# Attention followed by a token and channel mixer: the transposed q and k leave PSUM in another order of elements

## The chip, the cores and the metric

One core of a Trainium2 chip runs the whole program. The metric is the device time of one execution in microseconds (us); less is better. TensorE (PE) multiplies, VectorE (DVE) and ScalarE (ACT) read its results out of PSUM and do the elementwise work, GpSimd (POOL) works in SBUF only, and SyncE (SP) issues the DMAs.

## What is computed

For 8 batches and 8 heads, 576 tokens, head size 64: causal attention with a decay, and then a mixer over tokens and over channels on the joined heads (512 channels).

```python
s_pos = np.maximum(s, 0.0)
cum = np.cumsum(s_pos, axis=-1)
bias = -(cum[:, :, :, None] - cum[:, :, None, :])
scores = np.where(causal, -1e9, q @ k.T / 8 + np.minimum(bias, 0.0))
attn = softmax(scores)
x = (attn @ v)                       # heads joined: (8, 576, 512)
h = relu(x.T @ w_tok1) @ w_tok2      # tokens mixed, 256 wide
u = x + h.T
out = u + relu(u @ w_ch1) @ w_ch2    # channels mixed, 1536 wide
```

## The kernel before, in words

The work falls into 32 pairs of heads (8 batches of 4 pairs), and a mixer per batch.

**A pair.** One DMA (line 405) loads q, another k, for two heads: token 6p + r lies in partition p at place r, so 96 partitions hold six tokens each. POOL (line 412; for batch 0 also ACT, 416, or DVE, 414) casts them to bf16. Six PE transposes of 96x96 (line 436) write the transposed k side by side into one PSUM tile, psc: column r * 96 + p holds token 6p + r. A copy brings it into kT in order of tokens, by ACT (line 446) or DVE (line 448). The same is done for q, except that two copies of 64 partitions each (line 456 on ACT, line 458 on DVE) put the two heads into the two halves of qT, whose other parts are zero. The second copy does not start before the first has ended. Then come the scores: nine matmuls of kT against qT (line 473) in seven pieces, each in a psc tile, an exp per part of a piece on ACT (line 481), a mask on the diagonal blocks on DVE (line 489), 30 small matmuls with v (line 510, AV below), a reciprocal (517) and a scaling (522) on DVE. Tiles psc_113 to psc_115 are three PSUM banks shared by the transposes and the score pieces; kT, qT and E have three tiles each.

**A mixer.** Matmuls of lines 603 and 623 with transposes of line 642 mix tokens; lines 669 (with a relu on ACT, 676, or DVE, 678) and 688 (with an add on DVE, 699) mix channels. They use three other PSUM banks, pmx_118 to pmx_120.

**The order.** Nothing is scheduled at run time. Every step is given to a planner with the engines that may do it and a duration per engine; the planner takes the steps one by one, always the one that can start first by its own clock, with ties (within 0.03 us) settled by a priority in which the token mixer (0) comes ahead of attention (1) and that ahead of the channel mixer (2). For PE, attention's AV comes ahead of scores and those ahead of transposes. The planner picks the engine, too: every copy of q and k may go to ACT or DVE. What it picks is written out as the fixed order of each engine's queue, and an engine whose next instruction has to wait holds up all behind it. The planner's duration for one copy of q or k is 0.55 us on ACT (`c_act(576)`) and 0.67 us on DVE (`c_dve(576)`); for a cast on POOL it is 0.10 us and 1.5 ns per element.

Of the kernel before, what the change touches and what calls it, by code (L numbers as in the profile page):

```python
# [9 lines left out]
BF16 = mybir.dt.bfloat16  # L10
# [190 lines left out]
def c_act(n, bias=False):  # L201
    occ = 0.07 + n * 0.000833 + (0.093 if bias else 0.0)
    return occ, occ + 0.22


def c_dve(n, two=False):
    occ = 0.07 + n * (0.00053 if two else 0.00104)
    return occ, occ + 0.22


def c_pool(n, per=0.0022):
    occ = 0.10 + n * per
    return occ, occ + 0.25
# [3 lines left out]
def kernel(  # L217
# [12 lines left out]
    nc = tc.nc  # L230

    B, H, S, D = q.shape
# [8 lines left out]
    R = 6  # L241
    PR = S // R
# [49 lines left out]
    P = Plan()  # L292
    count = [0]

    def seq():
        count[0] += 1
        return count[0]
# [73 lines left out]
    def stage_v(b):  # L371
        vf, vp = Buf(r_vf), Buf(r_vp)
        vbuf[b] = vp
        for c in range(NJ):
            n = min(128, S - c * 128)

            def load(c=c, n=n):
                nc.sync.dma_start(out=vf.t[0:n, c, :, :],
                                  in_=v[b, :, c * 128 : c * 128 + n, :].rearrange("h p d -> p h d"))
            P.op({"SP": (0.6, 0, load)}, writes=[(vf, c)], prio=seq(), dma=1024 * 0.02 / 16 * n / 128)  # L380
        for c in range(NJ):
            n = min(128, S - c * 128)

            def mul(eng, c=c, n=n):
                eng.tensor_tensor(  # L385
                    out=vp.t[0:n, c, :, 0:D], in0=vf.t[0:n, c, :, :],
                    in1=wT[0:n, c, b * H : b * H + H].unsqueeze(2).to_broadcast([n, H, D]), op=ALU.mult)
            alts = ({"DVE": (*c_dve(512), lambda mul=mul: mul(nc.vector))} if b == 0 else
                    {"POOL": (*c_pool(512), lambda mul=mul: mul(nc.gpsimd))})
            P.op(alts, reads=[(vf, c), "wT"], writes=[(vp, c)], prio=b * 10 + 5 if b else 0)  # L390

        def ones():
            nc.gpsimd.tensor_copy(out=vp.t[:, 0 : NJ - 1, :, D], in_=wT[:, 0 : NJ - 1, b * H : b * H + H])
            nc.gpsimd.tensor_copy(out=vp.t[0:64, NJ - 1, :, D], in_=wT[0:64, NJ - 1, b * H : b * H + H])
        P.op({"POOL": (0.5, 0.7, ones)}, reads=["wT"], writes=[(vp, "w")], prio=b * 10 + 5)
# [3 lines left out]
    def stage_qk(b, h):  # L399
        for buf, src in (("k", k), ("q", q)):  # L400
            f, n = Buf(r_qf), Buf(r_qn)
            qkn[(buf, b, h)] = n

            def load(f=f, src=src):
                nc.sync.dma_start(out=f.t[:, :, :, :].rearrange("p e r d -> p e (r d)"),
                                  in_=src[b, h : h + 2, :, :].rearrange("e (p r) d -> p e (r d)", r=R))
            P.op({"SP": (0.6, 0, load)}, writes=[(f, 0)], prio=seq(), dma=192 * 0.064 / 16)

            def cast(e, f=f, n=n):
                i = f.t[:, :, :, :].rearrange("p e r d -> p r e d")  # L410
                if e == 0:
                    nc.gpsimd.tensor_copy(out=n.t[:, :, :, :], in_=i)
                elif e == 1:
                    nc.vector.tensor_copy(out=n.t[:, :, :, :], in_=i)
                else:
                    nc.scalar.copy(out=n.t[:, :, :, :], in_=i)
            alts = {"POOL": (*c_pool(768, 0.0015), lambda cast=cast: cast(0))}
            if b == 0:
                alts["DVE"] = (*c_dve(768), lambda cast=cast: cast(1))
                alts["ACT"] = (*c_act(768), lambda cast=cast: cast(2))  # L420
            P.op(alts, reads=[(f, 0)], writes=[(n, 0)], prio=b * 10 + h)
# [3 lines left out]
    def pair(b, h):  # L425
        pi = b * H + h
        qn, kn = qkn[("q", b, h)], qkn[("k", b, h)]
        qT, kT, E = Buf(r_qT), Buf(r_kT), Buf(r_E)
        pr = (1, pi)
        for nat, dst in ((kn, kT), (qn, qT)):  # L430
            pt = Buf(r_sc, False)

            def tr(nat=nat, pt=pt):
                o = pt.t[:, :].bitcast(BF16)
                for r in range(R):
                    nc.tensor.transpose(out=o[:, r * PR : (r + 1) * PR],
                                        in_=nat.t[:, r, :, :].rearrange("p e d -> p (e d)"), identity=ident[0:PR, 0:PR])
            P.op({"PE": (R * 0.045, R * 0.045 + 0.3, tr)}, reads=[(nat, 0)], writes=[(pt, 0)], holds=[dst], prio=(1, pi, 2))

            def un(p0, p1, pt=pt):  # L440
                return pt.t[p0:p1, :].bitcast(BF16)[:, 0 : R * PR].rearrange("d (r p) -> d r p", r=R)
            if dst is kT:
                def evk(eng, un=un):
                    o = kT.t[:, 0:S].rearrange("d (p r) -> d r p", r=R)
                    if eng == 0:
                        nc.scalar.copy(out=o, in_=un(0, 128))
                    else:
                        nc.vector.tensor_copy(out=o, in_=un(0, 128))
                P.op({"ACT": (*c_act(576), lambda evk=evk: evk(0)), "DVE": (*c_dve(576), lambda evk=evk: evk(1))},
                     reads=[(pt, 0)], writes=[(kT, 0)], prio=1)  # L450
            else:
                for hh in range(2):
                    def evq(eng, hh=hh, un=un):
                        o = qT.t[hh * 64 : hh * 64 + 64, hh, :].rearrange("d (p r) -> d r p", r=R)
                        if eng == 0:
                            nc.scalar.copy(out=o, in_=un(hh * 64, hh * 64 + 64))  # L456
                        else:
                            nc.vector.tensor_copy(out=o, in_=un(hh * 64, hh * 64 + 64))  # L458
                    P.op({"ACT": (*c_act(576), lambda evq=evq: evq(0)),
                          "DVE": (*c_dve(576), lambda evq=evq: evq(1))},  # L460
                         reads=[(pt, 0)], writes=[(qT, hh)], prio=1)
        for pc, piece in enumerate(PIECES):
# [14 lines left out]
            for (jc, a, e, c0) in cols:  # L477
# [6 lines left out]
                if a == jc * 128:  # L484
                    n = min(128, S - a)
# [46 lines left out]
    def load_w(slot, n, dma_fn, dst, key, us):  # L532

        st = stage[slot]
        P.op({"SP": (0.6, 0, lambda: dma_fn(st))}, writes=[("st", slot)], prio=seq(), dma=us)

        def cast(e):
            for (d, i) in dst(st):
                if e == 0:
                    nc.gpsimd.tensor_copy(out=d, in_=i)  # L540
                elif e == 1:
                    nc.vector.tensor_copy(out=d, in_=i)
                else:
                    nc.scalar.copy(out=d, in_=i)
        P.op({"POOL": (*c_pool(n, 0.0015), lambda: cast(0)), "DVE": (*c_dve(n), lambda: cast(1)),
              "ACT": (*c_act(n), lambda: cast(2))}, reads=[("st", slot)], writes=[key], prio=3)

    def load_tok():
# [19 lines left out]
    def load_ch1(mc):  # L568
        load_w((2, 3, 0, 1)[mc], DC,
               lambda st: nc.sync.dma_start(out=st[:, :], in_=moe_w_ch1[mc * 128 : mc * 128 + 128, :]),  # L570
               lambda st: [(wc1[:, mc, :], st[:, :])], ("wc1", mc), 2.1)
# [84 lines left out]
    def chan(b, u, us, uT):  # L656
# [26 lines left out]
        for c in range(5 if odd else 4):  # L683
# [20 lines left out]
            P.op({"SP": (0.6, 0, st)}, reads=[(o, 0)], prio=0, dma=128 * 0.088 / 16)  # L704

    stage_qk(0, 0)
    stage_v(0)
    for h in range(2, H, 2):
        stage_qk(0, h)
    load_tok()  # L710
    for i in range(4):
        load_ch1(i)
    stage_qk(1, 0)
    stage_v(1)
    for i in range(4):
        load_ch2(i)
    for h in range(2, H, 2):
        stage_qk(1, h)
    for b in range(2, B):
        stage_v(b)  # L720
        for h in range(0, H, 2):
            stage_qk(b, h)
# [46 lines left out]
```

## Time and profile before

| | |
|---|---|
| two runs | 476.28 and 479.09 us, median 477.68 |
| profiled execution, its own time | 477.95 us |
| its span in the trace | 476.3 us, 7665 instructions |
| busy: PE, ACT, DVE, POOL | 370.4, 310.5, 251.4, 94.0 us |
| granted TensorE clock, mean | 0.903 of full speed |

The span is what the trace covers; 1.65 us of the execution lie outside it. Busy shares are averages over two unlike stages: up to about 346 us pairs and mixers are interleaved, after that only mixers are left. Which wait ends last in a stage is told by the chain of work, which is followed back from the last instruction.

### The profile page before, as it was taken

What the parts mean: (1) busy time and instruction counts of PE and PEld (TensorE: products, weight loads), DVE (VectorE), ACT (ScalarE), POOL (GpSimd) and SP (SyncE); (2) the same over time, 40 slices, a digit from 0 to 9 for tenths busy, and PEclk for the clock granted to TensorE, in tenths of its full rate; (3) what the DMA queues carried; (4) which work ended last, traced back from release to release, by engine and by line L of the source; (5) the groups of instructions that cost most, each with busy time, mean ns of one, the idle gap of its engine ahead of it and who ended that gap; (6) DMA issues with size and microseconds to landing.
All of it is one profiled execution on the core that took longest, in us unless ns stands there. A gap on an engine that the chain in (4) does not pass through costs nothing.

```text
span 476.3 us, 7665 instructions
## 1 busy us (share of the span) xinstructions
PE 370.4 (78%) x2949; PEld 206.2 (43%) x2949; DVE 251.4 (53%) x498; ACT 310.5 (65%) x504; POOL 94.0 (20%) x129
## 2 busy tenths in 40 slices
PE   1547648686596696597677586788999999999996
PEld 1324314343343554363424343434764446544562
DVE  7958886664555877672557746735603213130102
ACT  4796776898668987786868769856651516325250
POOL 1453821332143215214304302100000000000000
PEclk9997969997788977787979979968999999999999
DMA  9999999272314806501322300001002010020202
GB/s 190 307 241 247 311 196 279 50 164 76 98 45 123 184 15 142 108 27 51 114 77 94 101 1 3 22 23 45 1 6 106 1 60 30 23 88 1 88 17 95
DMA packets 59172, 45.86 MB, mean 96 GB/s; under 512 B 39296, under 2 KB 52160, under 8 KB 59136
## 3 DMA queue, kind: packets, MB, share of 16 engines
q1 hardware_dynamic: 59136, 45.38, 36.4%
q8 instruction: 23, 0.38, 0.3%
q14 instruction: 13, 0.11, 0.1%
HBM read 35.93 MB, written 9.44 MB: 95 GB/s over the span
## 4 chain that ended last, share of the span: by engine, by line
PE 56%; ACT 21%; DVE 18%; issue 4%; ACTq 0%; DVEq 0%
PE pmx_119 L669 7%; PE pmx_120 L688 7%; PE pmx_118 L669 7%; PE pmx_118 L688 6%; PE pmx_120 L669 6%; PE pmx_119 L688 6%; ACT qT_79 L456 5%; ACT qT_81 L456 4%; DVE qT_79 L458 4%; ACT qT_80 L456 4%; PE psc_113 L473 3%; DVE qT_80 L458 3%; PE psc_114 L473 3%; DVE qT_81 L458 3%; PE psc_115 L473 2%
## 5 line engine op out<-in xcount | busy, mean ns | idle before, releaser
L669 PEld LDWEIGHTS <-wc_67 128*128 128x128 bf16 x576 | 58.6, 103 | 45.9 <-issue 10.6
L688 PEld LDWEIGHTS <-gb_108 128*128 128x128 bf16 x240 | 23.6, 100 | 27.3 <-issue 2.4
L489 DVE TENSOR_TENSOR E_86<-E_86,keep 128x256 bf16<-128x256 bf16 (+1 forms) x55 | 21.3, 405 | 18.2 <-ACT E_86 L481 18.1
L688 PEld LDWEIGHTS <-ga_107 128*128 128x128 bf16 x192 | 19.6, 104 | 25.2 <-issue 8.3
L489 DVE TENSOR_TENSOR E_87<-E_87,keep 128x256 bf16<-128x256 bf16 (+1 forms) x50 | 15.3, 321 | 25.4 <-ACT E_87 L481 25.2
L669 PE MATMUL pmx_119<-uTb_106,wc_67 128*128 128x320 bf16 x136 | 26.5, 321 | 0.0
L473 PEld LDWEIGHTS <-kT_83 128*128 128x128 bf16 x99 | 10.1, 110 | 36.9 <-issue 30.5
L385 POOL TENSOR_TENSOR vp_91<-vf_89,wT 128x512 bf16<-128x512 f32 (+1 forms) x20 | 20.5, 1046 | 26.5 <-PE pav_117 L510 22.5
L473 PEld LDWEIGHTS <-kT_84 128*128 128x128 bf16 x90 | 9.4, 112 | 36.5 <-issue 29.7
L669 PE MATMUL pmx_118<-uTb_106,wc_67 128*128 128x320 bf16 x132 | 25.0, 315 | 0.0
L473 PEld LDWEIGHTS <-kT_82 128*128 128x128 bf16 x99 | 9.6, 107 | 31.7 <-issue 26.3
L688 PE MATMUL pmx_118<-wc_68,gb_108 128*128 128x512 bf16 x84 | 22.5, 413 | 0.0
L473 PE MATMUL psc_113<-qT_80,kT_83 128*128 128x512 bf16 (+1 forms) x30 | 11.9, 397 | 13.5 <-ACT qT_80 L456 9.1
L669 PE MATMUL pmx_120<-uTb_106,wc_67 128*128 128x320 bf16 x116 | 21.8, 313 | 0.0
L489 DVE TENSOR_TENSOR E_85<-E_85,keep 128x256 bf16<-128x256 bf16 (+1 forms) x55 | 15.8, 305 | 10.2 <-ACT E_85 L481 10.1
L473 PE MATMUL psc_113<-qT_81,kT_84 128*128 128x128 bf16 (+2 forms) x35 | 10.7, 373 | 13.5 <-ACT qT_79 L456 7.3
L458 DVE COPY qT_80<-psc_115 64x576 bf16<-64x576 bf16 x7 | 14.6, 2080 | 11.9 <-ACT qT_80 L456 9.0
L688 PE MATMUL pmx_120<-wc_68,ga_107 128*128 128x512 bf16 x84 | 20.5, 380 | 0.0
L676 ACT ACTIVATE ga_107<-pmx_120 128x512 bf16<-128x512 f32 x15 | 9.0, 602 | 17.5 <-PE pmx_120 L669 17.3
L688 PE MATMUL pmx_120<-wc_68,gb_108 128*128 128x512 bf16 x84 | 19.9, 379 | 0.0
L473 PE MATMUL psc_115<-qT_81,kT_84 128*128 128x512 bf16 (+2 forms) x31 | 10.7, 376 | 11.9 <-DVE qT_81 L458 7.0
L676 ACT ACTIVATE gb_108<-pmx_120 128x320 bf16<-128x320 f32 x24 | 10.5, 437 | 13.9 <-PE pmx_120 L669 11.9
(285 smaller groups left out, 986.6 us busy)
## 6 DMA issues: line engine op xcount, KB each, us to landing
gb_108<-in_moe_w_ch_dram SPq DMA_DIRECT2D x6, 768.0 KB, 9.5
vf_88<-in_v_dram SPq DMA_DIRECT2D x16, 256.0 KB, 5.3
vf_89<-in_v_dram SPq DMA_DIRECT2D x16, 256.0 KB, 6.1
qkf_69<-in_k_dram SPq DMA_DIRECT2D x11, 288.0 KB, 3.7
qkf_70<-in_q_dram SPq DMA_DIRECT2D x11, 288.0 KB, 4.2
qkf_71<-in_k_dram SPq DMA_DIRECT2D x11, 288.0 KB, 4.4
qkf_72<-in_q_dram SPq DMA_DIRECT2D x11, 288.0 KB, 4.6
qkf_73<-in_k_dram SPq DMA_DIRECT2D x10, 288.0 KB, 5.3
```

Of the source, the lines that this page charges most:

```text
L385: eng.tensor_tensor(out=vp.t[0:n, c, :, 0:D], in0=vf.t[0:n, c, :, :], in1=wT[0:n, c, b * H : b * H + H].unsqueeze(2).to_broadcast([n, H, D ...
L456: nc.scalar.copy(out=o, in_=un(hh * 64, hh * 64 + 64))
L458: nc.vector.tensor_copy(out=o, in_=un(hh * 64, hh * 64 + 64))
L473: nc.tensor.matmul(out=o[:, :, c0 : c0 + e - a], lhsT=kT.t[:, jc * 128 : jc * 128 + 128], rhs=qT.t[:, :, a:e], start=True, stop=True)
L489: nc.vector.tensor_tensor(out=E.t[:, :, d0 : d0 + n], in0=E.t[:, :, d0 : d0 + n], in1=keep[:, 0:n].unsqueeze(1).to_broadcast([128, 2, n]), ...
L669: nc.tensor.matmul(out=pm.t[:, 0 : e - a], lhsT=wc1[:, m, cc * 128 : cc * 128 + 128], rhs=uT.t[:, m, a:e], start=(m == 0), stop=(m == NMC ...
L676: lambda cc=cc, pm=pm, a=a, e=e: nc.scalar.activation(out=g.t[:, cc, a:e], in_=pm.t[:, 0 : e - a], func=AF.Relu),
L688: nc.tensor.matmul(out=pm.t[:, :], lhsT=g.t[:, cc, c * 128 : c * 128 + 128], rhs=wc2[:, cc, :], start=(cc == 0), stop=(cc == NCC - 1))
```

## The change

The copies of lines 446, 448, 456 and 458 walk over the same elements in another order. Before, the six runs of 96 columns are read as they lie in PSUM, and each element is written six elements (12 bytes) behind the last one. After, kT and qT are written from the first token to the last without gaps, and PSUM is read with a step of 96 elements (192 bytes), six reads per token group. Three of the planner's durations for POOL change with it: the casts of q, k and of the weights from 1.5 to 1.0 ns per element, the products with v from 2.2 to 1.9.

```diff
-                    {"POOL": (*c_pool(512), lambda mul=mul: mul(nc.gpsimd))})
+                    {"POOL": (*c_pool(512, 0.0019), lambda mul=mul: mul(nc.gpsimd))})
...
-            alts = {"POOL": (*c_pool(768, 0.0015), lambda cast=cast: cast(0))}
+            alts = {"POOL": (*c_pool(768, 0.0010), lambda cast=cast: cast(0))}
...
-                return pt.t[p0:p1, :].bitcast(BF16)[:, 0 : R * PR].rearrange("d (r p) -> d r p", r=R)
+                return pt.t[p0:p1, :].bitcast(BF16)[:, 0 : R * PR].rearrange("d (r p) -> d p r", r=R)
             if dst is kT:
                 def evk(eng, un=un):
-                    o = kT.t[:, 0:S].rearrange("d (p r) -> d r p", r=R)
+                    o = kT.t[:, 0:S].rearrange("d (p r) -> d p r", r=R)
...
-                        o = qT.t[hh * 64 : hh * 64 + 64, hh, :].rearrange("d (p r) -> d r p", r=R)
+                        o = qT.t[hh * 64 : hh * 64 + 64, hh, :].rearrange("d (p r) -> d p r", r=R)
...
-        P.op({"POOL": (*c_pool(n, 0.0015), lambda: cast(0)), "DVE": (*c_dve(n), lambda: cast(1)),
+        P.op({"POOL": (*c_pool(n, 0.0010), lambda: cast(0)), "DVE": (*c_dve(n), lambda: cast(1)),
```

Since the planner sees other durations, it writes out another order from the second pair on. On DVE, in the second and third pair of batch 0 (tiles numbered 80 and 81 are their qT, E_86 the second pair's exponentials, w_0 a weight of the token mixer), this is the difference:

```order
-L458 COPY qT_80<-psc_114 64x6x96
-L448 COPY kT_84<-psc_115 128x6x96
+L458 COPY qT_80<-psc_114 64x576
+L448 COPY kT_84<-psc_115 128x576
+L458 COPY qT_81<-psc_113 64x576 x2
 L489 TENSOR_TENSOR E_86<-E_86,keep 128x2x128
 L542 CAST w_0_64<-ga_107 128x1024
 L542 CAST w_0_64<-ga_107 64x256
-L489 TENSOR_TENSOR E_86<-E_86,keep 128x2x128 x3
-L489 TENSOR_TENSOR E_86<-E_86,keep 128x2x64
-L458 COPY qT_81<-psc_114 64x6x96
-L458 COPY qT_79<-psc_113 64x6x96
```

Both halves of the third pair's q now stand on DVE, ahead of the second pair's masks; before, one half stood behind them and the other on ACT.

On ACT, near row 142 of its queue, where one pair's last exp (E_86) and the next pair's exps (E_87) stand, before:

```order
L481 ACTIVATE E_86<-psc_113 128x2x64
L456 COPY qT_81<-psc_115 64x6x96
L446 COPY kT_82<-psc_114 128x6x96
L456 COPY qT_79<-psc_113 64x6x96
L481 ACTIVATE E_87<-psc_115 128x2x256
```

And at the same row in the changed kernel:

```order
L481 ACTIVATE E_86<-psc_114 128x2x64
L481 ACTIVATE E_87<-psc_115 128x2x256
L481 ACTIVATE E_87<-psc_113 128x2x256
L481 ACTIVATE E_87<-psc_114 128x2x64
L481 ACTIVATE E_87<-psc_114 128x2x192
```

The three copies that stood between the two pairs' exps have moved: the half of q that belongs to E_87 stands ten rows earlier, the k and q of the pair after it eight rows later. Over the program, ACT has 22 copies of k and 37 of q before, 23 and 32 after; DVE has 10 and 27 before, 9 and 32 after. On PE the number of channel-mixer matmuls behind the last AV is the same in both, 352 of line 669 and 276 of line 688.

## Rows read from the trace of the kernel before

**Rows 1.** Chain that ended last, 0 to 346 us, by line
```profile
by line: ACT qT_79 L456 6.6%; ACT qT_81 L456 6.1%; DVE qT_79 L458 5.4%; ACT qT_80 L456 5.4%; issue 4.6%; PE psc_113 L473 4.4%; PE pmx_119 L669 4.3%; DVE qT_80 L458 4.3%; PE pmx_118 L669 4.3%; PE psc_114 L473 3.9%; DVE qT_81 L458 3.5%; PE ps
```
**Rows 2.** Chain in order of time: start us, us, what
```profile
31.10 1.92 ACT kT_82 L446
...
121.81 0.27 PE psc_115 L436 x6
122.08 0.02 issue
122.11 2.12 ACT qT_81 L456
124.23 0.02 issue
124.25 2.07 DVE qT_81 L458
126.32 0.03 issue
126.35 2.07 DVE qT_79 L458
...
128.51 2.07 ACT qT_79 L456
...
289.29 0.66 ACT kT_83 L446
```
**Rows 3.** Windows: each engine's busy time (and count), granted clock, DMA share, GB/s
```profile
12.00:48.00 36.00, 21.25 (x206) 12.24 (x206) 27.25 (x52) 28.54 (x47) 15.00 (x17) 0.91 1.13 266
...
200.00:250.00 50.00, 36.86 (x315) 20.21 (x315) 25.70 (x59) 38.55 (x60) 11.71 (x15) 0.80 0.23 68
...
346.00:476.30 130.30, 125.28 (x701) 66.19 (x698) 26.87 (x42) 46.69 (x95) 0.00 (x0) 1.00 0.12 47
```
**Rows 4.** Lines 456, 458, 446: copies by tile, ns min/median/max, first and last start
```profile
L456 ACT COPY qT_81<-psc_115 x8: 2061/2092/2121, 58.3 to 307.3; 64x576 bf16<-64x576 bf16 x8
...
L458 DVE COPY qT_80<-psc_115 x7: 2069/2081/2096, 49.1 to 324.2; 64x576 bf16<-64x576 bf16 x7
...
L446 ACT COPY kT_83<-psc_113 x8: 2057/2116/2339, 20.3 to 289.3; 128x576 bf16<-128x576 bf16 x8
```
**Rows 5.** Other reads of PSUM, same columns
```profile
L650 ACT COPY uTa_105<-pmx_119 x3: 585/592/667, 57.4 to 396.7; 128x512 bf16<-128x512 bf16 x3
...
L652 DVE COPY uTb_106<-pmx_120 x4: 418/422/425, 106.2 to 371.6; 128x512 bf16<-128x512 bf16 x4
...
L676 ACT ACTIVATE gb_108<-pmx_118 x25: 437/437/653, 171.2 to 459.2; 128x320 bf16<-128x320 f32 x25
...
L676 ACT ACTIVATE ga_107<-pmx_119 x11: 597/597/605, 78.4 to 435.5; 128x512 bf16<-128x512 f32 x11
...
L678 DVE TENSOR_SCALAR gb_108<-pmx_118 x8: 478/488/492, 162.3 to 339.4; 128x320 bf16<-128x320 f32 x8
...
L678 DVE TENSOR_SCALAR ga_107<-pmx_119 x4: 684/688/692, 74.4 to 286.2; 128x512 bf16<-128x512 f32 x4
...
L517 DVE RECIPROCAL rc_96<-pav_117 x16: 183/185/196, 19.8 to 340.0; 128x5 f32<-128x5 f32 x16
```
**Rows 6.** Windows over stretches in which only copies stand on the chain
```profile
9.20:13.27 4.07, 0.77 (x5) 0.71 (x6) 3.26 (x2) 1.96 (x2) 0.00 (x0) 1.00 1.17 233
122.11:130.58 8.47, 3.00 (x48) 1.86 (x45) 5.22 (x6) 6.08 (x3) 2.37 (x3) 0.82 0.45 137
...
324.24:328.42 4.18, 2.50 (x14) 1.26 (x13) 3.29 (x3) 3.90 (x2) 0.00 (x0) 1.00 0.16 62
```
**Rows 7.** Chain again: groups of four PE matmuls at two durations
```profile
70.99 1.71 PE pmx_118 L669 x4
...
153.20 1.07 PE pmx_119 L669 x4
...
204.30 1.07 PE pmx_118 L669 x4
...
215.85 2.09 ACT kT_82 L446
...
218.56 1.71 PE pmx_118 L688 x4
...
224.54 0.86 PE pmx_118 L688 x4
...
316.71 1.71 PE pmx_119 L688 x4
```

## The prediction

> **What bounds the kernel now.** I read the chain of waits first, cut at 346 us, because the last AV ends near there and the order of PE behind it is the same in both kernels. Up to that point the copies of q hold 18.1% of the chain on ACT and 13.2% on DVE [rows 1]: of 346 us that is 62.6 and 45.7 us. The copies of k hold little, because they run beside the transposes of q: ten pieces, the first and last of which are shown [rows 2], 11.2 us on ACT and 5.2 on DVE. Together 124.7 us of the span hang on copies, and none lies behind 329 us.
>
> The pieces in order of time show how [rows 2]: six transposes of 0.27 us, then one half of q on ACT, the other half on DVE, then the next pair's halves, 8.47 us without a piece of PE. The windows come next. The stretch behind 346 us is PE's: 125.28 of 130.30 us busy at the full clock [rows 3]. Nothing in the change reaches it, so it stays 130 us. In the interleaved part no engine is full (200 to 250 us: PE 36.9, ACT 38.6, DVE 25.7 of 50 us), so it is latency that bounds it, and the longest latency is the copy.
>
> **What one copy costs now.** All 96 copies have medians of 2.06 to 2.3 us, the same on ACT and DVE, for 64 and for 128 partitions [rows 4]. The engines' own rates differ: ACT reads 320 columns of PSUM in 437 ns and 512 in 597, 0.83 ns a column over 170 ns; DVE takes 488 and 688, 1.04 ns a column over about 155 [rows 5]. At these rates 576 columns are 0.65 us on ACT and 0.75 on DVE. Since both engines come to 3.3 ns an element instead, the limit is no engine but the access. Of its two sides the read is innocent: line 650 reads bf16 from PSUM just as these copies do, without a step, and its 512 columns take 592 ns [rows 5]. What is left is the write with a step of 12 bytes.
>
> **What it will cost.** The new write has no gaps, which line 650 prices. The new read takes one element per 192 bytes of PSUM, which no long instruction of this trace does. From below: ACT 0.65 us; DVE 0.46 us if it takes two elements at a time as line 652 does (422 ns for 512) [rows 5], which I do not count on since neighbours in the new order are not neighbours in PSUM. From above: the reciprocal of line 517 reads five elements 264 bytes apart and takes 185 ns [rows 5], 25 ns more than five columns at DVE's rate; put wholly on the step, that is 5 ns an element more, and a copy would be 0.75 + 2.88 = 3.6 us. I take 0.65 and 0.75 us, since a reciprocal can well be slower than a copy by 25 ns of its own, and the bulky rows all lie at the engines' rates.
>
> [...]
>
> **The sum.** It is made against the profiled execution's own 477.95 us, which is 0.27 above the median of the two runs.
> - Copies on ACT: the chain has 62.6 + 11.2 = 73.8 us of them; a mean copy of 2.15 us becomes 0.65, so 70% goes: -51.5.
> - Copies on DVE: 45.7 + 5.2 = 50.9 us; 2.09 becomes 0.75, so 64% goes: -32.6. That makes 393.9.
> - PE works under the copies, too, and this cover shrinks. The copies on the chain form 26 stretches (three are shown, the first and the last among them [rows 6]), 124.8 us long, with 47.7 us of PE in them. Shortened to 0.325 of its length, a stretch like 122.11 to 130.58 leaves 2.75 us for 3.00 us of PE. Where PE's work is the longer, PE becomes what is late next; over the 26 stretches this adds up to +11.0.
> - [...] Granted clock is 0.80 from 200 to 250 us, and 1.00 once PE no longer waits [rows 3]. With waits of 1.4 us where 4.2 stood I count these groups at the full level: 10 x 0.85 + 9 x 0.53 = -13.3. Between none of it and, with the score matmuls that lie among them, twice as much.
> - The order: the half of q that DVE now does without a handover from ACT, and the copies that no longer stand between two pairs' exps, save or cost a wait here and there; the hold-ups by a queue's head scale with the copies, which the planner now prices nearly right (0.55 and 0.67 us). I put this at 0, with 10 us either way.
> - The durations for POOL change no instruction. POOL has 94 us of work off the chain, and its casts are prepared ahead: 0.
>
> 393.9 + 11.0 - 13.3 = 391.6; I say 391. Its own range is 368 (the clock twice, the order at its best) to 412.
>
> **The rivals.**
> 1. The read with a step pays half of what the write paid: a mean copy of 1.4 us. The chain holds 124.7 / 2.1 = 59 copies, each 0.7 shorter: -41, so 437. For it speaks that the step is far greater than before; against it that nothing in the trace shows a read from PSUM above the engines' rates, save 25 ns of a reciprocal. [...]
> 2. The front runs out of data. From 12 to 48 us the DMA engines are full (266 GB/s [rows 3]); six of the 26 stretches, 28.7 us of copies, lie before 85 us. If loads take the place of what goes there, some 19 us are given back: 410.
> 3. The change does not do what it says, since the read pays all that the write paid: 2.1 us a copy, no change, 478. The order alone is left, and the copies are as badly priced as before.
> 4. The other side: a read with a step is dearer than a write with one. By the reciprocal's 5 ns a copy is 3.6 us, and 59 x 1.5 us = 89 come on top: 566. It decides from a mean copy of 2.25 us on, where 59 x 0.16 passes 2%, about 9.6 us, which is what a measurement of this kernel tells from no change.
>
> **How the numbers follow.** Forecast 0.63, rival 1 0.18, rival 2 0.08, rival 3 0.05, rival 4 0.06. Faster by over 2% is the sum of the first three, 0.89; within 2% rival 3, 0.05; slower 0.06. The range runs from 360, below the forecast's own as the clock's and the order's bounds allow, to 440, which takes in rivals 1 and 2; rivals 3 and 4 and the tails are left out.
>
> **What would show it.** Lines 446 and 456 near 0.65 us and lines 448 and 458 near 0.75; copies under 15% of the chain up to the last AV, with PE's matmuls and the exps of line 481 in their place; the last AV near 261 us and 130 us of mixers behind it; a granted clock above 0.9 from 50 us on. A copy above 1 us would prove the price wrong; copies at 0.7 us with the last AV behind 285 us would prove the chain wrong.

## The result and the profile after

The changed kernel takes 374.48 us (373.98 and 374.98), the one before 477.68: a ratio of 0.784, 95% interval 0.773 to 0.795. The profiled execution took 374.98 us, its span is 373.2. The forecast was 391 us with a range of 360 to 440; 87 us of gain were expected and 103 came.

The copies, by tile, with their shortest, median and longest duration in ns, answer to [rows 4]:

```profile
L446 ACT COPY kT_84<-psc_113 x5: 632/632/639, 114.1 to 210.5; 128x576 bf16<-128x576 bf16 x5
...
L456 ACT COPY qT_79<-psc_114 x7: 615/633/634, 9.1 to 221.9; 64x576 bf16<-64x576 bf16 x7
...
L458 DVE COPY qT_79<-psc_114 x9: 736/750/760, 9.8 to 221.1; 64x576 bf16<-64x576 bf16 x9
```

2.08 us have become 0.63 on ACT and 0.75 on DVE: each engine is back at its own rate [rows 5], to within 20 ns of the two values that the forecast took. The windows answer to [rows 3]:

```profile
12.00:48.00 36.00, 28.34 (x301) 16.79 (x299) 28.08 (x67) 28.70 (x64) 20.12 (x24) 0.95 1.11 275
48.00:100.00 52.00, 46.21 (x469) 27.17 (x469) 39.38 (x90) 39.45 (x86) 21.11 (x25) 0.97 1.14 249
...
150.00:200.00 50.00, 48.15 (x501) 28.41 (x500) 36.71 (x88) 38.51 (x89) 22.79 (x29) 1.00 0.37 113
...
243.00:373.20 130.20, 124.15 (x692) 65.26 (x690) 26.87 (x42) 45.76 (x93) 0.00 (x0) 0.99 0.12 47
```

The last AV now ends near 239 us instead of 343. Behind it stand 134 us of mixers, where 133 stood before: the whole gain lies in the interleaved part. PE was busy for 37 of 50 us there (200 to 250 us [rows 3]); now it is busy for 48 (150 to 200 us), with the clock granted in full (1.00, against 0.80 in those 50 us of before). The chain up to 243 us, by line, answers to [rows 1], and the four pieces of DMA on it to nothing that was there before:

```profile
by line: DMA gb_108<-in_moe_w_ch_dram 5.6%; PE pmx_118 L688 5.0%; PE psc_114 L473 4.6%; PE pmx_120 L669 4.6%; PE psc_115 L473 4.5%; PE pmx_119 L669 4.4%; PE pmx_120 L688 4.3%; PE psc_113 L473 4.0%; DMA qkf_73<-in_k_dram 3.9%; PE pmx_118 L66
...
26.06 6.15 DMA vf_89<-in_v_dram
44.65 7.30 DMA gb_108<-in_moe_w_ch_dram
52.15 9.52 DMA qkf_73<-in_k_dram
72.49 6.40 DMA gb_108<-in_moe_w_ch_dram
```

No copy is left among the large shares; summed over all pieces the copies hold 25 us of 243, where it was 125 of 346. The largest shares are now PE's matmuls and, up to 79 us, 29.4 us of loads. In microseconds PE's pieces have shrunk as well, from 150 to 135.

### The profile page after: what moved, and what is told of

The parts are those of the page before. It is cut to its first block, busy times and chain, and to the rows that moved or that the text cites. A ratio compares the mean times of both kernels' runs of the same rounds, so it can differ in the third digit from the quotient of the medians.

```text
span 373.2 us, 7668 instructions
## 1 busy us (share of the span) xinstructions
PE 340.0 (91%) x2949; PEld 198.0 (53%) x2949; DVE 207.2 (56%) x498; ACT 228.3 (61%) x504; POOL 93.5 (25%) x129
## 4 chain that ended last, share of the span: by engine, by line
PE 68%; DVE 13%; DMA 8%; ACT 7%; issue 2%; POOL 1%; SPq 0%; ACTq 0%; DVEq 0%; POOLq 0%
PE pmx_118 L688 9%; PE pmx_120 L688 8%; PE pmx_120 L669 8%; PE pmx_119 L669 7%; PE pmx_118 L669 7%; PE pmx_119 L688 6%; DMA gb_108<-in_moe_w_ch_dram 4%; PE psc_114 L473 3%; PE psc_115 L473 3%; PE psc_113 L473 3%; DMA qkf_73<-in_k_dram 3%; PE pmx_119 L603 2%; PE pav_117 L510 2%; DVE ua_101 L630 2%; PE pav_116 L510 2%
## 5 line engine op out<-in xcount | busy, mean ns | idle before, releaser
L669 PEld LDWEIGHTS <-wc_67 128*128 128x128 bf16 x576 | 55.7, 98 | 37.4 <-issue 1.9
L688 PEld LDWEIGHTS <-gb_108 128*128 128x128 bf16 x240 | 23.1, 98 | 26.3 <-issue 0.4
L688 PEld LDWEIGHTS <-ga_107 128*128 128x128 bf16 x192 | 18.3, 97 | 19.8 <-issue 0.5
L489 DVE TENSOR_TENSOR E_86<-E_86,keep 128x256 bf16<-128x256 bf16 (+1 forms) x55 | 18.6, 355 | 11.3 <-ACT E_86 L481 10.9
L489 DVE TENSOR_TENSOR E_87<-E_87,keep 128x256 bf16<-128x256 bf16 (+1 forms) x50 | 18.9, 391 | 9.7 <-ACT E_87 L481 9.2
L489 DVE TENSOR_TENSOR E_85<-E_85,keep 128x256 bf16<-128x256 bf16 (+1 forms) x55 | 22.3, 425 | 3.6 <-ACT E_85 L481 3.3
L669 PE MATMUL pmx_119<-uTb_106,wc_67 128*128 128x320 bf16 x132 | 23.3, 299 | 0.0
L669 PE MATMUL pmx_120<-uTb_106,wc_67 128*128 128x320 bf16 x132 | 23.3, 299 | 0.0
L669 PE MATMUL pmx_118<-uTb_106,wc_67 128*128 128x320 bf16 x120 | 21.2, 299 | 0.0
L688 PE MATMUL pmx_118<-wc_68,ga_107 128*128 128x512 bf16 x84 | 20.6, 379 | 0.0
L688 PE MATMUL pmx_118<-wc_68,gb_108 128*128 128x512 bf16 x84 | 20.1, 379 | 0.0
L688 PE MATMUL pmx_120<-wc_68,gb_108 128*128 128x512 bf16 x84 | 19.9, 379 | 0.0
L676 ACT ACTIVATE gb_108<-pmx_120 128x320 bf16<-128x320 f32 x26 | 11.4, 437 | 13.9 <-PE pmx_120 L669 11.9
L676 ACT ACTIVATE gb_108<-pmx_119 128x320 bf16<-128x320 f32 x27 | 11.9, 439 | 12.9 <-PE pmx_119 L669 10.7
L669 PE MATMUL pmx_120<-uTa_105,wc_67 128*128 128x512 bf16 x76 | 19.5, 379 | 0.0
L481 ACT ACTIVATE E_85<-psc_115 128x128 bf16<-128x128 f32 (+2 forms) x37 | 15.8, 462 | 3.7 <-PE psc_115 L473 3.7
L481 ACT ACTIVATE E_86<-psc_114 128x512 bf16<-128x512 f32 (+2 forms) x36 | 15.8, 467 | 3.3 <-PE psc_114 L473 2.8
L481 ACT ACTIVATE E_85<-psc_113 128x512 bf16<-128x512 f32 (+2 forms) x31 | 15.3, 511 | 3.4 <-PE psc_113 L473 3.4
L688 PE MATMUL pmx_119<-wc_68,gb_108 128*128 128x512 bf16 x72 | 16.8, 379 | 0.0
L481 ACT ACTIVATE E_86<-psc_115 128x512 bf16<-128x512 f32 (+2 forms) x28 | 14.1, 520 | 3.9 <-PE psc_115 L473 3.9
```

Of the source, the lines that this page charges most:

```text
L481: nc.scalar.activation(out=E.t[:, :, d0 : d0 + e - a], in_=i[:, :, c0 : c0 + e - a], func=AF.Exp, scale=0.125)
L489: nc.vector.tensor_tensor(out=E.t[:, :, d0 : d0 + n], in0=E.t[:, :, d0 : d0 + n], in1=keep[:, 0:n].unsqueeze(1).to_broadcast([128, 2, n]), ...
L669: nc.tensor.matmul(out=pm.t[:, 0 : e - a], lhsT=wc1[:, m, cc * 128 : cc * 128 + 128], rhs=uT.t[:, m, a:e], start=(m == 0), stop=(m == NMC ...
L676: lambda cc=cc, pm=pm, a=a, e=e: nc.scalar.activation(out=g.t[:, cc, a:e], in_=pm.t[:, 0 : e - a], func=AF.Relu),
L688: nc.tensor.matmul(out=pm.t[:, :], lhsT=g.t[:, cc, c * 128 : c * 128 + 128], rhs=wc2[:, cc, :], start=(cc == 0), stop=(cc == NCC - 1))
```

## The experiments

The change has two parts which the diff mixes: the access of the copies, and three planner durations that set a new order. The planner is not told how the copies walk, so the parts can be had one by one. Four runs shared one chip; their ratios are against the kernel before on that chip.

**The access alone, in the order of before.**

```diff
-                    {"POOL": (*c_pool(512, 0.0019), lambda mul=mul: mul(nc.gpsimd))})
+                    {"POOL": (*c_pool(512), lambda mul=mul: mul(nc.gpsimd))})
...
-            alts = {"POOL": (*c_pool(768, 0.0010), lambda cast=cast: cast(0))}
+            alts = {"POOL": (*c_pool(768, 0.0015), lambda cast=cast: cast(0))}
...
-        P.op({"POOL": (*c_pool(n, 0.0010), lambda: cast(0)), "DVE": (*c_dve(n), lambda: cast(1)),
+        P.op({"POOL": (*c_pool(n, 0.0015), lambda: cast(0)), "DVE": (*c_dve(n), lambda: cast(1)),
```

> The new access with the planner's old durations for POOL, so that the order of every engine is the one of before. If the access makes the whole gain and the order nothing: 372 to 380 us, copies at 0.63 and 0.75 us. If the 17 us by which the change beat the forecast come from the new order: 388 to 395 us, the sum of the forecast without its order term (391).

Measured: 371.68 us, ratio 0.778 (0.775 to 0.781). The access makes the whole gain in an order that is word for word that of before. So the surplus over the forecast is not the order's. This run is also the cleanest pair to before, since nothing but the copies differs. Its busy times, its chain up to 240 us by line (buffer numbers left out), and two of its windows:

```profile
PE 342.2 (92%) x2949; PEld 198.5 (53%) x2949; DVE 213.4 (57%) x498; ACT 227.4 (61%) x504; POOL 96.4 (26%) x129
...
by line: PE psc L473 13.9%; PE pmx L669 13.3%; PE pmx L688 12.2%; DVE E L489 9.5%; PE pav L510 7.6%; PE pmx L603 7.3%; DVE qT L458 5.1%; ACT E L481 4.4%; ACT qT L456 2.9%; PE psc L436 2.8%; DVE ua L630 2.5%; issue 2.0%; DVE x L522 2.0%; DVE
...
150.00:200.00 50.00, 48.44 (x517) 29.06 (x515) 38.79 (x91) 38.64 (x89) 21.98 (x28) 1.00 0.38 110
...
240.00:372.10 132.10, 127.09 (x714) 67.46 (x711) 26.87 (x42) 48.18 (x98) 0.00 (x0) 1.00 0.12 46
```

The q copies hold 5.1% and 2.9% of 240 us, 19.2 us, where they held 108.3. At 0.7 us that is some 27 copies; before, it was 52.

**The order alone, with the long copies.** The changed kernel with the three patterns as before.

```diff
-                return pt.t[p0:p1, :].bitcast(BF16)[:, 0 : R * PR].rearrange("d (r p) -> d p r", r=R)
+                return pt.t[p0:p1, :].bitcast(BF16)[:, 0 : R * PR].rearrange("d (r p) -> d r p", r=R)
...
-                    o = kT.t[:, 0:S].rearrange("d (p r) -> d p r", r=R)
+                    o = kT.t[:, 0:S].rearrange("d (p r) -> d r p", r=R)
...
-                        o = qT.t[hh * 64 : hh * 64 + 64, hh, :].rearrange("d (p r) -> d p r", r=R)
+                        o = qT.t[hh * 64 : hh * 64 + 64, hh, :].rearrange("d (p r) -> d r p", r=R)
```

> The old access, copies of 2.1 us, in the new order that follows from the new durations for POOL. If the order makes nothing by itself: 470 to 485 us. If the order carries some 17 us: 457 to 463 us.

Measured: 471.22 us, ratio 0.985 (0.981 to 0.990). The new POOL durations are worth 6.5 us, or 1.5%, while the copies are long. With short copies they are worth nothing or cost a little: 374.48 us with them (375.90 in a later run), 371.68 without, though not side by side.

**k alone, or q alone, written with the step again.** In the changed kernel, the last diff applied to kT's copies or to qT's.

> The changed kernel with k alone written with the step again (32 of 96 copies at 2.1 us, same order). If the price of a copy is its place on the chain, as the forecast has it (16.4 of 124.7 us of copies): 11 us more, 383 to 390 us. If every copy costs alike wherever it stands, a third of the gain goes: 405 to 412 us.

> The changed kernel with q alone written with the step again (64 of 96 copies). By the chain (108.3 of 124.7 us): 73 to 90 us more, 447 to 465 us. If every copy costs alike, two thirds of the gain of 103 us go: 440 to 446 us.

Measured: k 388.39 us (ratio 0.812, 0.810 to 0.815), q 464.32 (0.972, 0.968 to 0.977). Against 374.48, k costs 13.9 us and q 89.8, together 103.7, where both at once cost 96.7 in the same order (471.22 less 374.48): the two overlap a little. A third of the copies makes 13% of the price, as their place on the chain says (16.4 of 124.7 us, 13%). The theory by which every copy counts alike falls. The trace of the kernel before shows why: in all 32 pairs the copy of k has ended at least 2.3 us before q's second copy, and in 28 of them the next score starts within 0.06 us of that second copy's end. The transposes of q, which the prediction names as the cover, take 0.27 us [rows 2] and hide little of a copy of 2.1 us; it is q's own two copies, one after the other, that outlast k's.

**Which side of the access is dear, and from which size on.** Two runs, with two and with three tokens written side by side before each step:

```diff
-                return pt.t[p0:p1, :].bitcast(BF16)[:, 0 : R * PR].rearrange("d (r p) -> d p r", r=R)
+                return pt.t[p0:p1, :].bitcast(BF16)[:, 0 : R * PR].rearrange("d (j t p) -> d j p t", t=2, p=PR)
...
-                    o = kT.t[:, 0:S].rearrange("d (p r) -> d p r", r=R)
+                    o = kT.t[:, 0:S].rearrange("d (p j t) -> d j p t", t=2, p=PR)
...
-                        o = qT.t[hh * 64 : hh * 64 + 64, hh, :].rearrange("d (p r) -> d p r", r=R)
+                        o = qT.t[hh * 64 : hh * 64 + 64, hh, :].rearrange("d (p j t) -> d j p t", t=2, p=PR)
```

> The changed kernel with kT and qT written in runs of two tokens (4 bytes), then a step of 12 bytes. If each separate run costs what each separate element did (3.3 ns): 288 runs, 0.96 us over a fixed 0.17, copies of 1.1 us on both engines, 395 to 410 us in all. If only pieces smaller than 4 bytes are dear: copies at the engines' rates, 0.65 and 0.75 us, and 370 to 378 us.

> The changed kernel with kT and qT written in runs of three tokens (6 bytes), then a step of 12 bytes. If the price is per run: 192 runs, 0.64 us over a fixed 0.17, copies of 0.8 us on both engines. If only pieces smaller than 4 bytes are dear, every run has one such piece: 192 x 3.3 ns and the pairs beside them at the engines' rates, some 1.0 us. 376 to 395 us in all.

The second has `t=3` in these lines. Measured, one execution each: 374.52 and 377.43 us. The copies of both, all tiles of a line together, first with runs of two and then of three:

```profile
L456 ACT COPY qT<-psc x32: 631/651/669, 9.1 to 222.1; 64x576 bf16<-64x576 bf16 x32
L458 DVE COPY qT<-psc x32: 740/760/761, 9.8 to 222.8; 64x576 bf16<-64x576 bf16 x32
```
```profile
L456 ACT COPY qT<-psc x32: 786/800/824, 9.1 to 224.8; 64x576 bf16<-64x576 bf16 x32
L458 DVE COPY qT<-psc x32: 777/806/824, 9.9 to 225.6; 64x576 bf16<-64x576 bf16 x32
```

Runs of 4 bytes already go at each engine's rate (0.65 and 0.76 us), with the same step of 12 bytes behind them, so a price per run falls. Runs of 6 bytes are a little dearer, 0.80 us on both engines: 0.17 us over ACT's 0.63 for 192 odd pieces of 2 bytes, or 0.9 ns each, where a lone piece cost 2.5 ns more than ACT's rate. The price per run had given this 0.8 us, but the runs of two refute it; the other theory had given 1.0. So how an odd piece beside a pair is priced stays open.

A third run takes the step away from the read, too; it leaves out the reordering of q's and k's tokens:

```diff
-                return pt.t[p0:p1, :].bitcast(BF16)[:, 0 : R * PR].rearrange("d (r p) -> d p r", r=R)
+                return pt.t[p0:p1, :].bitcast(BF16)[:, 0 : R * PR]
...
-                    o = kT.t[:, 0:S].rearrange("d (p r) -> d p r", r=R)
+                    o = kT.t[:, 0:S]
...
-                        o = qT.t[hh * 64 : hh * 64 + 64, hh, :].rearrange("d (p r) -> d p r", r=R)
+                        o = qT.t[hh * 64 : hh * 64 + 64, hh, :]
```

> The changed kernel with the copies reading and writing 576 columns without any step; this leaves out the reordering of q's and k's tokens. If the read with a step costs nothing: ACT's copies stay at 0.63 us, DVE's fall to 0.46 us if it can now take two elements at a time, and since PE bounds the kernel now, 370 to 376 us. If the read costs something on ACT, its copies fall below 0.60 us. If copies still bound the kernel, 41 DVE copies at 0.3 us less give 362 to 368 us.

Measured: 369.29 us, ratio 0.775 (0.767 to 0.782), and these copies:

```profile
L446 ACT COPY kT<-psc x23: 632/638/683, 16.2 to 215.4; 128x576 bf16<-128x576 bf16 x23
...
L458 DVE COPY qT<-psc x32: 440/460/463, 9.8 to 217.7; 64x576 bf16<-64x576 bf16 x32
```

ACT does not notice the step of 192 bytes in its read: 0.63 us with and without. DVE loses 0.3 us by it: without the step (0.46 us) it goes at the rate of line 652, with it (0.75 us) at that of line 678 [rows 5], half as fast. And 41 shorter copies on DVE move the whole by 1.4%, with intervals that overlap: little is left to win from the copies in this order. This run also closes the question of the side. In the kernel before, the copies read without a step, too, and only their write was another: 2.08 us there, 0.63 on ACT and 0.46 on DVE here.

**Could an order have hidden the long copies?** The kernel before, old access and old POOL durations, with the one false price put right:

```diff
-                P.op({"ACT": (*c_act(576), lambda evk=evk: evk(0)), "DVE": (*c_dve(576), lambda evk=evk: evk(1))},
+                P.op({"ACT": (2.1, 2.32, lambda evk=evk: evk(0)), "DVE": (2.1, 2.32, lambda evk=evk: evk(1))},
...
-                    P.op({"ACT": (*c_act(576), lambda evq=evq: evq(0)),
-                          "DVE": (*c_dve(576), lambda evq=evq: evq(1))},
+                    P.op({"ACT": (2.1, 2.32, lambda evq=evq: evq(0)),
+                          "DVE": (2.1, 2.32, lambda evq=evq: evq(1))},
```

> The kernel before, copies of 2.1 us and all, but the planner told so (2.1 us on ACT and DVE in place of 0.55 and 0.67), which moves the order of all engines. If the loss came from the wrong price, since work that waits stood at the head of the queues: 400 to 440 us. If it came from the copies' length itself, which no order hides with three score tiles in PSUM: 455 to 475 us.

Measured: 388.13 us, ratio 0.813 (0.808 to 0.818), better than either range. This was the surprise of the study: 89 of the 103 us come without any shorter copy. Its chain over the whole span, by line, two copy lines, and one of PE's waits (us in total, times, longest):

```profile
by line: PE pmx L688 21.9%; PE pmx L669 16.2%; PE psc L473 7.7%; ACT qT L456 6.9%; DVE qT L458 5.8%; PE pmx L603 3.9%; PE pav L510 3.4%; ACT kT L446 2.9%; DVE E L489 2.7%; ACT E L481 2.6%; issue 2.6%; DMA qkf<-in_q_dram 1.8%; DVE ub L630 1.
...
L456 ACT COPY qT<-psc x34: 2061/2082/2343, 9.1 to 303.6; 64x576 bf16<-64x576 bf16 x34
L458 DVE COPY qT<-psc x30: 2052/2084/2118, 17.8 to 301.5; 64x576 bf16<-64x576 bf16 x30
...
PE psc L473 <- ACT qT L456: 11.1, 9, 2.5
```

The copies are as long as ever. But a planner that knows it puts 646 of the mixer's large matmuls between the pairs' last transposes and their first scores, where the order of before has 244, so PE works while the copies run. Scores waited for q's copies for 68.5 us in the kernel before, in 28 waits; here they do so for 12.4 us, in 11. The two longest groups of before:

```profile
PE psc_115 L473 <- DVE qT_79 L458: 10.2, 4, 3.5
PE psc_113 L473 <- ACT qT_79 L456: 9.8, 4, 3.2
```

That matmuls are there to be had is seen at the other end: 184 of line 669 and 168 of line 688 stand behind the last AV, not 352 and 276.

**What is left to win.** Four runs on one chip: the changed kernel again, the last order with the new access, and the changed kernel with the planner told 2.1 us for a copy, or the true 0.64 and 0.76.

> The changed kernel once more, on the chip of the three runs beside it: 372 to 377 us. If the access alone is really the faster of the two (371.7 us in its own run), this stays above 373.

> The order of the run in which the planner had 2.1 us for a copy, now with the new access (copies of 0.63 and 0.75 us); the POOL durations are the old ones. If that order already hides most of a long copy, so that the copy's length is worth little in it: 370 to 380 us, 8 to 18 us under the 388.1 of the same order with long copies. If the two gains add, which TensorE's 340 us of work forbid: far below 360.

> The changed kernel with the planner told 2.1 us for a copy that takes 0.63 or 0.75. More matmuls of the mixer stand between a pair's transposes and its scores (184 of line 669 behind the last AV, not 352). If PE is the bound: 366 to 376 us. If the longer spread between transposes and scores holds the score tiles too long: 376 to 390.

> The changed kernel with the planner told what the trace shows, 0.64 us on ACT and 0.76 on DVE (0.55 and 0.67 before). The order changes on all engines, the durations do not. If PE is the bound and the price is near enough: 370 to 377 us, not to be told from the changed kernel.

```diff
-                P.op({"ACT": (*c_act(576), lambda evk=evk: evk(0)), "DVE": (*c_dve(576), lambda evk=evk: evk(1))},
+                P.op({"ACT": (0.64, 0.86, lambda evk=evk: evk(0)), "DVE": (0.76, 0.98, lambda evk=evk: evk(1))},
...
-                    P.op({"ACT": (*c_act(576), lambda evq=evq: evq(0)),
-                          "DVE": (*c_dve(576), lambda evq=evq: evq(1))},
+                    P.op({"ACT": (0.64, 0.86, lambda evq=evq: evq(0)),
+                          "DVE": (0.76, 0.98, lambda evq=evq: evq(1))},
```

| run | us | ratio to before | interval |
|---|---|---|---|
| changed kernel | 375.90 | 0.787 | 0.782 to 0.792 |
| copies priced 2.1, new access, old POOL durations | 369.63 | 0.775 | 0.771 to 0.779 |
| changed kernel, copies priced 2.1 | 372.59 | 0.781 | 0.777 to 0.785 |
| changed kernel, copies priced 0.64 and 0.76 | 368.91 | 0.773 | 0.770 to 0.777 |

In the order that hides them, copies of 0.7 us in place of 2.1 are worth 18.5 us (388.13 to 369.63; two chips), where they are worth 106 in the order of before. The gains of access and order do not add: both fill the same idle time of PE. The true price has the lowest time and beats the changed kernel by 1.9%, with intervals apart; I had expected 370 to 377 us and no difference that can be told. From the second row of the table it is not told apart, since the intervals overlap. All four lie within 2% of each other, and of the true price's run these are the windows:

```profile
12.00:48.00 36.00, 28.30 (x303) 17.22 (x302) 28.27 (x67) 29.39 (x67) 21.63 (x25) 1.00 1.10 275
48.00:100.00 52.00, 46.64 (x476) 27.51 (x484) 40.64 (x90) 37.08 (x83) 24.35 (x28) 0.97 1.09 255
100.00:240.00 140.00, 135.57 (x1456) 87.04 (x1471) 106.56 (x266) 109.38 (x257) 48.67 (x62) 1.00 0.38 102
```

PE is busy for 135.6 of 140 us from 100 us on. Most of what may still be open to an order lies before that, where PE idles for 13 of 88 us and the DMA engines are full (shares of 1.10 and 1.09); no run tried it.

## Why the prediction was right, and where it was off

**What a copy costs** was right, from both ends: 0.63 and 0.75 us, against 0.65 and 0.75. The argument that the write is the guilty side, drawn from line 650, holds by the runs of two (0.65 and 0.76 us a copy) and by the run without a step. 192 bytes between elements of PSUM cost ACT nothing (0.63 us with the step and without). Rivals 1, 3 and 4 fall.

**The copies' terms, -51.5 and -32.6, held for the pieces that they count, but the chain hides others.** Without its order term the forecast is 391.6 us, and the run with the access alone took 371.7 (its profiled execution 373.8). That run has the order of before, so every instruction on the chain of before can be looked up in it. The copies among them sum to 40.6 us where they were 124.5: -83.9, against -84.1 in the sum. But 9.5 us more of that chain are copies under another name: seven pieces called "issue" (time in which an engine waits for nothing that the profile shows) lie inside a copy that is running on that engine. Two of them, in the chain and then in the queue of ACT:

```profile
287.84 1.45 issue
289.29 0.66 ACT kT_83 L446
289.94 1.26 issue
...
287.57 2.09 ACT L456 COPY qT_79<-psc_115 64x576 bf16<-64x576 bf16 x1
289.29 2.30 ACT L446 COPY kT_83<-psc_113 128x576 bf16<-128x576 bf16 x1
```

In the run with the access alone at most 1.4 us of these seven are left. The sum left them at their old length, which makes 8 of the 18 us between 391.6 and 373.8; the other 10 lie in the next two terms. That this run's own chain has only 21 us of copies gives nothing on top. With the same order and the same waits the old chain must still be gone through, so its length at the new durations is a floor for the time; a copy leaves the chain only where other work lasts as long. Most of that is DVE's, whose instructions other than copies rise on the chain from 29 to 59 us (the masks of line 489 from 8 to 23), while PE's pieces fall from 150 to 142.5.

**PE under the copies, +11.0, and the clock, -13.3.** PE's instructions on the old chain, up to the last AV, take 147.0 us in before and 128.8 in the run with the access alone: -18.2 where the clock's term has -13.3, within its bound of twice that. The term takes 0.85 us off each of ten groups of four 512-column matmuls (nine at 1.71 us, one at 1.65) and 0.53 us off each of nine groups of 320 columns (1.07 us) [rows 7], and leaves out the scores. No run shows these 13.3 us by themselves. What the runs showed in their place: in before, the granted clock is 0.50 over 18 of the 19 groups and 0.56 over the one of 1.65 us, where it is 1.00 over groups that take 0.86 us (at 224.54 [rows 7]) and 0.54 us (at 172.23). On the changed kernel's chain no such group is left at 1.71 or 1.07 us; two lie between the levels (1.53 and 1.02 us). PE's busy time up to the last AV shows it, too: 245 us in before (370.4 less 125.3), 215 in the run with the same order (342.2 less 127.1 behind 240 us), at a granted clock of 0.80 from 200 to 250 us before [rows 3] and 1.00 from 150 to 200 us in that run. Copies, hidden copies and PE together make -110, while the two spans differ by 104.2 us (476.3 and 372.1). So, as an estimate by difference, 6 to 8 us came back as new waits, where the sum has +11.0; no run shows them by themselves.

**The order, 0 with 10 us either way**, held for the order that this change writes: -6.5 us with long copies, some +3 with short ones. Its reason holds as far as it goes: with short copies, the new order won nothing over that of before. What the prediction did not ask is whether another order could have hidden long copies; the run with the true long price shows that it could. So the loss needs both, long copies and an order made for short ones, and taking away either one brings most of the gain. The reading that latency bounds the kernel was right, but the latency cost so much because of where it stood, not because nothing was there to put under it.

**Rival 2, the front**, came true in part without moving the result. Loads hold 29.4 us of the changed kernel's chain before 79 us, and the DMA engines are full to 100 us (shares of 1.11 from 12 us and 1.14 from 48 us on). The run with the access alone has no load on its chain and is about as fast, so the loads stand level with other waits there.

## What to carry to other kernels

The sign was a copy that took the same time on two engines with different rates (2.08 us, where the rates give 0.65 and 0.75): its access held it up. The narrowest piece that it wrote was the cause (2 bytes; with 4 it took 0.65 and 0.76 us), and the remedy was to move the step to the side that reads PSUM (0.63 and 0.75 us). The durations in a planner (or in the head of whoever writes an order) belong to the kernel as much as its instructions do: check them against the trace first. Copies of 2.1 us cost 106 us in an order that priced them at a quarter to a third of their length, and 18.5 in one that knew it. And the chain says well which copies matter (13% for k, 87% for q). For the size of the gain, look inside its "issue" pieces as well, and add what every other instruction on it loses, here PE's (147.0 us of them in before, 128.8 with the access alone), whose granted clock rose from 0.80 (200 to 250 us) to 1.00 (150 to 200 us).

## What the runs showed of the hardware

- Writes of lone 2-byte elements with a step of 12 bytes took 3.3 ns an element on ACT and DVE alike (2.08 us for 576). Pairs of 4 bytes with the same step went at the engines' rates (0.65 and 0.76 us for 576), and runs of three took 0.80 us on both.
- A bf16 read of PSUM with a step of 192 bytes cost ACT nothing (0.63 us for 576 columns with and without). On DVE it took 0.75 us where the read without a step took 0.46.
